# Lightning attention and an MLP on one Trainium2 core: plain row- and column-tiled attention for the first four chunks, and a static order planned for later landings of the early loads

## Chip, cores and metric

The kernel runs on one core of a Trainium2 chip. The metric is the device time of one execution in microseconds; lower is better. Time before: 229.05 us, the median of five runs (228.29 to 230.45).

## What is computed

Decayed linear attention over 4 batches, 8 heads, 768 positions and head size 64, followed by a two-layer MLP (512 to 2048 to 512) on the 3072 tokens that come out of it. The reference, cut to what matters:

```python
for b in range(nb):                       # blocks of 64 positions
    intra = np.einsum('bhic,bhjc->bhij', qb, kb) * Dmask[None]     # lam ** (i - j) for i >= j
    intra = np.einsum('bhij,bhjd->bhid', intra, vb)
    inter = np.einsum('bhid,bhde->bhie', qb * lam_pow[None], kv_state)
    out[:, :, sl] = intra + inter
    kv_state = lam_block[None, :, None, None] * kv_state + np.einsum('bhsd,bhse->bhde', kb * rev_pow[None], vb)
x = attn_out.transpose(0, 2, 1, 3).reshape(B * S, H * D)
h = x @ w_in
g = np.where(h >= 1, h, np.where(h <= -1, 0.0, (h + 1) ** 2 / 4))
return g @ w_out
```

## The kernel before

**Attention.** The 3072 tokens are 24 chunks of 128 tokens (c = 0 to 23), six to a batch; c0 or k0, q0, v0 below mean chunk 0 and its three loads. For each chunk the kernel loads k, q and v (each 128x512 f32, 256 KB), casts k and q to bf16 (`cast`, L246 on ACT, L248 on DVE for chunk 0), and multiplies v by a table of decays on POOL (`cast_v`, L252, into `vn`). TensorE then transposes k and q into one PSUM tile `pt` (`f_t`, L268). `f_kb` (L274) copies the transposed k out, `f_qT` (L278) multiplies the transposed q by the decay table `tab_q` (four pieces per two chunks, L141). The scores come in two steps g = 0 and 1: `f_s` (L294) is the product of k and q into the one PSUM tile `ps`, `f_m` (L300) multiplies by the causal mask into `sc`. `f_o` (L307, L310) adds the state's part and the scores times v into `po`, `f_x` (L317) casts `po` into a quarter of `xT`. `f_u` (L284) and `f_ub` (L288) keep the running state.

Two heads share the 128 partitions. To work on both with full-width matmuls the kernel lays k and v out block-diagonally: `kbd` and `vi` are zeroed once, and each chunk's data is written into the diagonal blocks, for `kbd` by two half-height copies, for `vi` by four small moves (`f_vb`: DVE copies at L260 for chunks 0 to 3, DMAs at L262 from POOL for chunks 4 to 11 and from SP behind them). Step g then covers the keys of one half of the chunk for both heads, so that step 1 needs only the later 64 queries.

**MLP.** The tokens are 6 stages of 512. `f_l1` (L327) is a group of 16 matmuls (or 8 twice as wide) of the first layer, 16 groups to a stage; `f_r` (L335) is the relu on ACT that empties its PSUM tile `ph` (two buffers); three DVE operations (L341, L345, L360) make `gT`; `f_l2` (L366) is a group of four 512-column matmuls of the second layer; `f_y` and `f_st` copy and store.

**The order.** Nothing is looped at run time. Every step is entered with `add(key, engine, ns, fn, needs, due, extra)`: its assumed duration, the time `extra` from its end until its result can be used, what it needs, and when it is due. `run_plan` then places the steps on the engines one by one, as a list scheduler does, and emits each engine's instructions in that order. On the chip each engine runs its own list in order; real waits come from data dependences alone. Where the plan leaves a gap on TensorE before the first l2, the kernel puts filler matmuls into the unused PSUM tile `spin` (L225).

**The loads.** A list `order` gives the sequence of chunk loads ("c") and of the eight weight pieces ("w": w0 to w3 are quarters of w_in, w4 to w7 of w_out; each 1 MB of f32, cast to bf16 by the DMA). Before, chunk 0's three loads and those of chunks 6 on are issued by SP, the weights and chunks 1 to 5 by POOL. The plan treats the DMA as one engine:

```python
add(key, "SP" if sp else "POOL", 600 if sp else 900 if kind == "c" else 800, fn, need, due=0, extra=1250 if sp else 930)
add(land, "DMA", ns, lambda: None, [key] + landed[-1:], extra=1000 if i < SW else 1500, due=0)
```

with ns = 2600 for a weight piece, 1060 for an SP load and 720 for a POOL load. The SP load of k of chunk 6 waits for the landing of w6 (`add_manual_dep`).

Of the kernel before, what the change touches and what calls it, by code (L numbers as in the profile page):

```python
# [8 lines left out]
F32 = mybir.dt.float32  # L9
# [14 lines left out]
def kernel(  # L24
# [30 lines left out]

    LD, RING = 6, 6
# [8 lines left out]
    scp = ctx.enter_context(tc.tile_pool(name="scp", bufs=3))  # L65
# [52 lines left out]
    nc.vector.memset(flat(kbd[0]), 0.0)  # L118
# [5 lines left out]
    nc.vector.tensor_scalar(causal, row[:, 0:128], late, None, op0=AX.is_ge)  # L124
    nc.vector.tensor_copy(row[:, 2 * C:], row_i[:, 2 * C:])
    for t in vi:
        nc.gpsimd.memset(flat(t), 0.0)  # L127
# [4 lines left out]
    ln_t = const.tile([128, HP], F32)  # L132
    for hi in range(2):
        nc.vector.tensor_copy(ln_t[64 * hi:64 * hi + 64], ln_lam[64 * hi:64 * hi + 64].rearrange("p (a b) -> p a b", b=2)[:, :, hi])
    tab_k = const.tile([128, NCB, H], F32)
    nc.scalar.activation(out=tab_k, in_=arg, func=AF.Exp, scale=-1.0)
# [35 lines left out]
    def run_plan(free):  # L172
# [14 lines left out]
        for x in reversed(topo):  # L187
            d = [u.due - u.ns - x.extra - LAT for u in users[x.key] if u.eng not in ("DMA", "SP")]
            x.due = min(d + ([x.own] if x.own is not None else []), default=1e9)
            if x.eng in ("DMA", "SP") or x.key[0] in ("l1", "l2", "li", "wi"):  # L190
                x.due = x.own
# [39 lines left out]
    def mm(*cols):  # L231
        return sum(c / 2.4 + 3 for c in cols)
# [24 lines left out]
    def f_vb(c, g, hi):  # L257
        o, i = vi[c % NV][HD[hi], :, g, hi, :], vn[c % NV][HD[g], :, hi, :]
        if c < CPS:
            nc.vector.tensor_tensor(o, i, i, op=AX.max)  # L260
        else:
            (nc.gpsimd if c < VP else nc.sync).dma_start(out=o, in_=i)  # L262
# [7 lines left out]
    KA = 2  # L270

    def f_kb(c, hi):
        e = nc.scalar.copy if c < KA else nc.vector.tensor_copy
        e(out=kbd[c % NKB][HD[hi], :, :, hi, :], in_=ptt[c][HD[hi], 1].rearrange("p a (b d) -> p a b d", b=2))  # L274
# [15 lines left out]
    def f_s(c, g):  # L290
        t = pp_s.tile([128, 4, 128], F32, name="ps", tag="ps")
        pst[c, g] = t if g == 0 else t[:, 0:2, :].rearrange("p a (b d) -> p (a b) d", b=2)
        for hp in range(HP):
            nc.tensor.matmul(pst[c, g][:, hp, :], lhsT=kbd[c % NKB][:, hp, g].rearrange("p a d -> p (a d)"),  # L294
                             rhs=qT[c][:, hp, 64 * g:], start=True, stop=True)

    def f_m(c, g):
        if g == 0:
            sc_sb[c] = [scp.tile([128, HP, n], BF16, name=f"sc{n}", tag=f"sc{n}") for n in (128, 64)]
        nc.vector.tensor_tensor(sc_sb[c][g], pst[c, g], _bc(causal[:, 0:128 - 64 * g], 1, HP), op=AX.mult)  # L300

    def f_o(c):
        cb = c % NCB
        po = pot[c] = pp_o.tile([128, HP, 128], F32, name="po", tag="po")
        for hp in range(HP):
            if cb > 0:
                nc.tensor.matmul(po[:, hp], lhsT=ubd[(c - 1) % NUB][:, hp, :], rhs=qT[c][:, hp, :],  # L307
                                 start=True, stop=False)
            for g in range(2):
                nc.tensor.matmul(po[:, hp, 64 * g:], lhsT=vi[c % NV][:, hp, g].rearrange("p a d -> p (a d)"),  # L310
                                 rhs=sc_sb[c][g][:, hp, :], start=(cb == 0 and g == 0), stop=(g == 1))
# [92 lines left out]
    def f_load(c, x):  # L404
        t = qkv_ld[c, x] = ld.tile([128, H, D], F32, name=f"x{x}f", tag=f"x{x}f")
        b, s0 = c // NCB, (c % NCB) * C
        e = nc.gpsimd if 0 < c < SW else nc.sync
        d = e.dma_start(out=t, in_=(q, k, v)[x][b, :, s0:s0 + C, :].rearrange("h p d -> p h d"))  # L408
        if c == SW and x == 1:
            tc.add_manual_dep(d.ins, w_dma[6].ins.name, SYNC)  # L410

    SW = 6
    order = [("c", 0), ("c", 1), ("w", 0), ("c", 2), ("w", 1), ("c", 3), ("w", 2), ("w", 3), ("w", 4), ("c", 4), ("w", 5), ("w", 6), ("c", 5), ("w", 7)]
    order += [("c", c) for c in range(6, NCH)]

    fifo, landed, splast = [], [], []
    for kind, i in order:
        for x in (1, 0, 2) if kind == "c" else (0,):
            sp = kind == "c" and not 0 < i < SW
            if kind == "w":  # L420
                key, land, ns, fn, need = ("wi", i), ("w", i), 2600, lambda i=i: load_w(i), []
            else:
                key, land, ns, fn = ("li", i, x), ("ld", i, x), 1060 if sp else 720, lambda i=i, x=x: f_load(i, x)
                need = [("cast", i - LD, x), ("w", 6) if i == SW else None]
# [8 lines left out]
            add(land, "DMA", ns, lambda: None, [key] + landed[-1:], extra=1000 if i < SW else 1500, due=0)  # L433
            landed.append(land)

    nz = {"kb": NKB, "ub": NUB, "vb": NV}
    for i in range(1, NKB):
        add(("z", "kb", i), "DVE", 540, lambda i=i: nc.vector.memset(flat(kbd[i]), 0.0))
    for i in range(NUB):
        add(("z", "ub", i), "DVE", 270, lambda i=i: nc.vector.memset(flat(ubd[i]), 0.0))  # L440

    for c in range(NCH):
        od, cb = o_due(c), c % NCB
        lastu = c - 1 if cb else c - 2
        for x in (1, 0):
            e = "DVE" if c == 0 else "ACT"
            add(("cast", c, x), e, 600 if e == "DVE" else 610, lambda c=c, x=x, e=e: cast(c, x, e),
                [("ld", c, x), ("t", c - 3), ("u", c - 3), ("cast", c - 1, x)])
        for hp in range(HP) if c < NCB and c % 2 == 0 else ():
            add(("tab", c, hp), "ACT", 410, lambda c=c, hp=hp: tabq(c, hp), [("tab", c, hp - 1)])  # L450
        add(("cast", c, 2), "POOL", 1060, lambda c=c: cast_v(c),
            [("ld", c, 2), ("o", c - NV), ("u", c - NV), ("cast", c - 1, 2)], due=-1)
        for i in range(4):
            need = [("cast", c, 2), ("o", c - NV), ("z", "vb", c)]
            if c < CPS:
                add(("vb", c, i), "DVE", 230, lambda c=c, i=i: f_vb(c, i // 2, i % 2), need)
            elif c < VP:
# [5 lines left out]
        for hi in range(2):  # L463
            add(("kb", c, hi), "ACT" if c < KA else "DVE", 480 if c < KA else 365, lambda c=c, hi=hi: f_kb(c, hi), [("t", c), ("s", c - NKB, 1), ("z", "kb", c)])
        add(("qT", c), "DVE", 690, lambda c=c: f_qT(c), [("t", c), ("o", c - 3), ("qT", c - 1)] + [("tab", c // 2 * 2, hp) for hp in range(HP) if c < NCB])
        if cb < NCB - 1:
            add(("u", c), "PE", mm(*[128] * 4), lambda c=c: f_u(c),
                [("cast", c, 1), ("cast", c, 2), ("ub", lastu, 0), ("ub", lastu, 1), ("u", lastu)], due=od - 6000, extra=FILL)
            for hi in range(2):
                add(("ub", c, hi), "ACT", 372, lambda c=c, hi=hi: f_ub(c, hi), [("u", c), ("o", c - NUB + 1), ("z", "ub", c)])  # L470
        for h in range(2):
            add(("s", c, h), "PE", mm(*[128 - 64 * h] * 4), lambda c=c, h=h: f_s(c, h),
                [("kb", c, 0), ("kb", c, 1), ("qT", c), ("m", c, 0) if h else ("m", c - 1, 1)],
                due=od - 5500 + 2000 * h, extra=FILL)
            add(("m", c, h), "DVE", 690 - 270 * h, lambda c=c, h=h: f_m(c, h), [("s", c, h), ("o", c - 3), ("m", c, 0) if h else None])
        add(("o", c), "PE", mm(*[128] * (8 if cb else 4), *[64] * 4), lambda c=c: f_o(c),
# [27 lines left out]
    run_plan({"PE": 5500, "ACT": 4900, "DVE": 4800, "POOL": 4100, "DMA": 2700, "SP": 800})  # L504
# [30 lines left out]
```

## Time and profile before

| | |
|---|---|
| median of 5 runs | 229.05 us (228.29 to 230.45) |
| the profiled execution | 230.45 us, its span 228.6 us |
| granted TensorE clock, mean | 0.993 |
| PE busy | 217.4 us (95%) |
| PE weight loads | 158.6 us (69%) |
| DVE / ACT / POOL busy | 161.8 / 138.4 / 70.3 us |
| HBM read / written | 27.27 / 6.29 MB |
| DMA, SP's hardware queue | 75,792 packets, 22.81 MB |
| DMA, POOL's software queue | 6,448 packets, 9.18 MB |
| filler matmuls (L225) | 37, 12.0 us |

The span runs from the first to the last instruction of the profiled execution; the rest of its time lies around it. Matmuls are pipelined and the profile counts each from issue to end, so PE can be busy without being at its peak. L numbers are lines of the kernel before.

### The profile page before, as it was taken

Reading aid. Unit: us, or ns where it says so; the run is one execution under the profiler, and the core shown is the slowest. Engines: PE = TensorE matmul, PEld = TensorE weight load, DVE = VectorE, ACT = ScalarE, POOL = GpSimd, SP = SyncE. Lnnn points to the kernel's source line nnn. Section 1 sums busy time; section 2 is a strip of 40 time slices with the busy share of each in tenths; the row PEclk is TensorE's granted clock in tenths of the full one; section 3 lists DMA queues with packets and bytes.
Section 4 is the critical chain, followed back from the end, with each engine's and each line's share of the span. In section 5 each row is a group of like instructions: output and inputs, shape, how many; then the busy total and the mean of one; then the engine's idle time right before and its main releaser. Section 6 shows DMA issues by size and latency. Waiting matters only on the chain.

```text
span 228.6 us, 5723 instructions
## 1 busy us (share of the span) xinstructions
PE 217.4 (95%) x2309; PEld 158.6 (69%) x2309; DVE 161.8 (71%) x295; ACT 138.4 (61%) x249; POOL 70.3 (31%) x91
## 2 busy tenths in 40 slices
PE   7679999999979999999999999999999999999993
PEld 2348898788667878787777677777777777766441
DVE  8785998985969995998577687584875775554300
ACT  3678785677777766767666567655565554545121
POOL 8987847666889140112011130000000000000000
PEclk9799999999999999999999999999999999999999
DMA  6999999999999999677975941112101101110212
GB/s 137 199 214 242 189 262 249 190 229 228 227 230 255 218 258 238 160 175 154 239 171 123 219 121 58 48 41 70 49 0 46 49 0 49 47 46 3 91 56 82
DMA packets 82410, 32.36 MB, mean 142 GB/s; under 512 B 73744, under 2 KB 77840, under 8 KB 82384
## 3 DMA queue, kind: packets, MB, share of 16 engines
q1 hardware_dynamic: 75792, 22.81, 40.7%
q0 software_dynamic: 6448, 9.18, 18.8%
q8 instruction: 18, 0.29, 0.5%
q14 instruction: 8, 0.07, 0.1%
q10 hardware_dynamic: 144, 0.00, 0.0%
HBM read 27.27 MB, written 6.29 MB: 147 GB/s over the span
## 4 chain that ended last, share of the span: by engine, by line
PE 75%; DMA 12%; POOL 7%; ACT 3%; issue 1%; DVE 0%; ACTq 0%; POOLq 0%
PE py L366 33%; PE ph L327 31%; DMA x1f<-in_k_dram 8%; DMA x2f<-in_v_dram 4%; PE pt L268 3%; PE ps L294 3%; PE po L310 3%; POOL vn L252 2%; PE po L307 1%; PE pu L284 1%; POOL x1f L408 1%; POOL x0f L408 1%; ACT r L335 1%; POOL vi L127 1%; POOL w_in_sb L154 1%
## 5 line engine op out<-in xcount | busy, mean ns | idle before, releaser
L327 PE MATMUL ph<-xT,w_in_sb 128*128 128x128 bf16 (+1 forms) x1152 | 98.9, 237 | 0.8 <-ACT xT L317 0.4
L366 PE MATMUL py<-w_out_sb,gT 128*128 128x512 bf16 x384 | 95.6, 379 | 0.0
L335 ACT ACTIVATE r<-ph,one 128x512 bf16<-128x512 f32 x96 | 65.4, 686 | 49.8 <-PE ph L327 36.4
L327 PEld LDWEIGHTS <-w_in_sb 128*128 128x128 bf16 x1152 | 81.6, 98 | 14.9 <-issue 1.3
L366 PEld LDWEIGHTS <-gT 128*128 128x128 bf16 x384 | 35.4, 98 | 27.7
L252 POOL TENSOR_TENSOR vn<-x2f,tab_k 128x512 bf16<-128x512 f32 x24 | 27.3, 1139 | 59.9 <-DMA vi<-vn 36.8
L341 DVE TENSOR_SCALAR t<-r 128x1024 bf16<-128x1024 bf16 x48 | 22.1, 461 | 31.9 <-ACT r L335 31.7
L345 DVE TENSOR_TENSOR w<-r,t 128x1024 bf16<-128x1024 bf16 x48 | 37.0, 771 | 1.3
L360 DVE TENSOR_TENSOR gT<-w,t 128x1024 bf16<-128x1024 bf16 x48 | 35.6, 741 | 1.3
L300 DVE TENSOR_TENSOR sc<-ps,causal 128x512 bf16<-128x512 f32 (+1 forms) x48 | 26.6, 554 | 9.6 <-PE ps L294 9.2
L371 ACT COPY osb<-py 128x512 f32<-128x512 f32 x24 | 14.0, 585 | 15.7 <-PE py L366 14.5
L274 DVE COPY kbd<-pt 64x512 bf16<-64x512 bf16 x44 | 18.4, 418 | 5.7 <-PE pt L268 5.3
L262 POOL DMA_DIRECT2D vi<-vn x32 | 20.2, 645 | 2.7 <-POOL vn L252 2.4
L294 PE MATMUL ps<-qT,kbd 128*128 128x128 bf16 (+1 forms) x192 | 16.2, 208 | 2.3 <-ACT kbd L274 1.2
L246 ACT CAST ks<-x1f 128x512 bf16<-128x512 f32 x23 | 14.2, 618 | 6.8 <-DMA x1f<-in_k_dram 4.6
L294 PEld LDWEIGHTS <-kbd 128*128 128x128 bf16 x192 | 12.6, 98 | 7.9 <-ACT kbd L274 2.6
L278 DVE TENSOR_TENSOR qT<-pt,tab_q 128x512 bf16<-128x512 bf16 x24 | 16.6, 691 | 0.7
L317 ACT CAST xT<-po 128x512 bf16<-128x512 f32 x24 | 14.0, 584 | 4.6 <-PE po L310 4.5
L288 ACT CAST ubd<-pu 64x256 bf16<-64x256 f32 x40 | 14.6, 365 | 2.8 <-PE pu L284 2.5
L310 PE MATMUL po<-sc,vi 128*128 128x128 bf16 x192 | 15.6, 206 | 0.3 <-DMA vi<-vn 0.3
L246 ACT CAST qs<-x0f 128x512 bf16<-128x512 f32 x23 | 14.2, 616 | 0.8 <-DMA x0f<-in_q_dram 0.8
L310 PEld LDWEIGHTS <-vi 128*128 128x128 bf16 x192 | 13.2, 98 | 1.6 <-DMA vi<-vn 0.5
(45 smaller groups left out, 130.4 us busy)
## 6 DMA issues: line engine op xcount, KB each, us to landing
out_dram<-osb SPq DMA_DIRECT2D x24, 256.0 KB, 2.0
x1f<-in_k_dram SPq DMA_DIRECT2D x19, 256.0 KB, 4.5
x0f<-in_q_dram SPq DMA_DIRECT2D x19, 256.0 KB, 4.5
x2f<-in_v_dram SPq DMA_DIRECT2D x19, 256.0 KB, 4.6
w_in_sb<-in_moe_w_in_dram POOLq DMA_DIRECT2D x4, 512.0 KB, 8.0
w_out_sb<-in_moe_w_out_dram POOLq DMA_DIRECT2D x4, 512.0 KB, 10.4
vi<-vn SPq DMA_DIRECT2D x48, 32.0 KB, 2.0
x1f<-in_k_dram POOLq DMA_DIRECT2D x5, 256.0 KB, 7.5
```

Source lines behind the costliest of these rows:

```text
L246: nc.scalar.copy(out=t, in_=qkv_ld[c, x])
L252: nc.gpsimd.tensor_tensor(vn[c % NV].rearrange("p a b d -> p (a b) d"), qkv_ld[c, 2], _bc(tab_k[:, c % NCB, :], 2, D), op=AX.mult)
L262: (nc.gpsimd if c < VP else nc.sync).dma_start(out=o, in_=i)
L294: nc.tensor.matmul(pst[c, g][:, hp, :], lhsT=kbd[c % NKB][:, hp, g].rearrange("p a d -> p (a d)"), rhs=qT[c][:, hp, 64 * g:], start=True, ...
L300: nc.vector.tensor_tensor(sc_sb[c][g], pst[c, g], _bc(causal[:, 0:128 - 64 * g], 1, HP), op=AX.mult)
L310: nc.tensor.matmul(po[:, hp, 64 * g:], lhsT=vi[c % NV][:, hp, g].rearrange("p a d -> p (a d)"), rhs=sc_sb[c][g][:, hp, :], start=(cb == 0 ...
L327: nc.tensor.matmul(ph[:, j * m:(j + 1) * m], lhsT=w_in_sb[:, ko, (i + j) * 128:(i + j + 1) * 128], rhs=xT[s][:, ko, p * m:(p + 1) * m], st ...
L335: nc.scalar.activation(out=r_t[grp][:, i, :], in_=ph_t[s, ni, part], func=AF.Relu, bias=one[:, 0:1])
L341: nc.vector.tensor_scalar(t_t[grp], r_t[grp], 0.5, 1.0, op0=AX.mult, op1=AX.min)
L345: nc.vector.tensor_tensor(w_t[grp], r_t[grp], t_t[grp], op=AX.subtract)
L360: nc.vector.tensor_tensor(o, w, t, op=AX.mult)
L366: nc.tensor.matmul(py_t[s, ms], lhsT=gT[s][:, ko, ms * 128:(ms + 1) * 128], rhs=w_out_sb[:, ko, :], start=(ko == 0), stop=(ko == FO - 1))
```

## The change

Chunks 0 to 3 (`PLAIN = 4`) no longer use the block-diagonal layout. Their transposed k is copied out as it stands (`kplain`, in one copy: ACT for chunk 0, DVE for 1 to 3), and step g of the scores is now head half g: four matmuls over 64 partitions (row-tiled) with all 128 queries. In `f_o` each pair of heads takes two matmuls with a 64-wide stationary operand straight from `vn`, into the two halves of the partitions of `po` (column-tiled). Their `vi` copies are gone, and both mask products are 128 wide, with a mask of their own (`plain`).

With that, the zeroing moves: `vi` is zeroed by POOL behind the cast of v1 instead of ahead of its first load, `kbd` by DVE after the last plain use, `ubd` in the preamble. The cast of `row` goes from DVE to ACT, `ln_t` is computed by ACT, `tab_k` is placed by the planner, and the later pieces of `tab_q` wait for kb of chunk 0 and x of chunk 1.

The load of v0 goes from SP to POOL, and so do those of chunk 6 (`SW = 7`). Chunk 4 stands ahead of w4, and w7 behind chunk 6; SP's first load behind them, k of chunk 7, waits for w7. The planner's durations, landing allowances and the engines' starting times change.

```diff
+    PLAIN, KA = 4, 1
...
-    nc.vector.memset(flat(kbd[0]), 0.0)
...
-    nc.vector.tensor_scalar(causal, row[:, 0:128], late, None, op0=AX.is_ge)
-    nc.vector.tensor_copy(row[:, 2 * C:], row_i[:, 2 * C:])
-    for t in vi:
-        nc.gpsimd.memset(flat(t), 0.0)
+    plain = const.tile([128, 128], F32)
+    for t, p in ((plain, pos[:, 0:1]), (causal, late)):
+        nc.vector.tensor_tensor(t, row[:, 0:128], ... p.to_broadcast([128, 128]), op=AX.is_ge)
+    for t in ubd:
+        nc.vector.memset(flat(t), 0.0)
+    nc.scalar.copy(out=row[:, 2 * C:], in_=row_i[:, 2 * C:])
...
-        if c < CPS:
-            nc.vector.tensor_tensor(o, i, i, op=AX.max)
-        else:
-            (nc.gpsimd if c < VP else nc.sync).dma_start(out=o, in_=i)
+        (nc.gpsimd if c < VP else nc.sync).dma_start(out=o, in_=i)
...
     def f_kb(c, hi):
-        e = nc.scalar.copy if c < KA else nc.vector.tensor_copy
-        e(out=kbd[c % NKB][HD[hi], :, :, hi, :], in_=ptt[c][HD[hi], 1].rearrange("p a (b d) -> p a b d", b=2))
+        if c < PLAIN:
+            (nc.scalar.copy if c < KA else nc.vector.tensor_copy)(out=kplain(c), in_=ptt[c][:, 1])
+        else:
+            nc.vector.tensor_copy(kbd[c % NKB][HD[hi], :, :, hi, :], ptt[c][HD[hi], 1].rearrange("p a (b d) -> p a b d", b=2))
+
+    def kplain(c):
+        return kbd[c % NKB][:, 0:2].rearrange("p a b c d -> p (a b c d)").rearrange("p (h k) -> p h k", k=128)
...
+        for i in range(4 if c < PLAIN else 0):
+            nc.tensor.matmul(t[:, i, :], lhsT=kplain(c)[HD[g], i, :], rhs=qT[c][HD[g], i, :], start=True, stop=True)
+        for hp in range(HP if c >= PLAIN else 0):
...
     def f_m(c, g):
+        if c < PLAIN:
+            t = scp.tile([128, HP, 128], BF16, name="sc128", tag="sc128")
+            sc_sb[c] = sc_sb.get(c, []) + [t]
+            nc.vector.tensor_tensor(t, pst[c, g], _bc(plain, 1, HP), op=AX.mult)
+            return
...
+            for hi in range(2 if c < PLAIN else 0):
+                nc.tensor.matmul(po[HD[hi], hp], lhsT=vn[c % NV][:, hp, hi, :], rhs=sc_sb[c][hi][:, hp, :],
+                                 start=(cb == 0), stop=True)
-            for g in range(2):
+            for g in range(2 if c >= PLAIN else 0):
...
-        e = nc.gpsimd if 0 < c < SW else nc.sync
+        e = nc.gpsimd if (c, x) > (0, 1) and c < SW else nc.sync
...
-            tc.add_manual_dep(d.ins, w_dma[6].ins.name, SYNC)
+            tc.add_manual_dep(d.ins, w_dma[7].ins.name, SYNC)
...
-    SW = 6
-    order = [("c", 0), ("c", 1), ("w", 0), ("c", 2), ("w", 1), ("c", 3), ("w", 2), ("w", 3), ("w", 4), ("c", 4), ("w", 5), ("w", 6), ("c", 5), ("w", 7)]
-    order += [("c", c) for c in range(6, NCH)]
+    SW = 7
+    order = [("c", 0), ("c", 1), ("w", 0), ("c", 2), ("w", 1), ("c", 3), ("w", 2), ("w", 3), ("c", 4), ("w", 4), ("w", 5), ("w", 6), ("c", 5), ("c", 6), ("w", 7)]
+    order += [("c", c) for c in range(7, NCH)]
...
-                key, land, ns, fn, need = ("wi", i), ("w", i), 2600, lambda i=i: load_w(i), []
+                key, land, ns, fn, need = ("wi", i), ("w", i), 2800, lambda i=i: load_w(i), []
...
-            add(land, "DMA", ns, lambda: None, [key] + landed[-1:], extra=1000 if i < SW else 1500, due=0)
+            add(land, "DMA", ns, lambda: None, [key] + landed[-1:], extra=950 if sp and i == 0 else 1000 if kind == "c" and i < 2 else 3500 if kind == "c" and i < SW else 2000, due=0)
...
+    for i in range(NKB):
+        last = max(c for c in range(PLAIN) if c % NKB == i)
+        add(("z", "kb", i), "DVE", 485, lambda i=i: nc.vector.memset(flat(kbd[i]), 0.0), [("s", last, 1)])
+    for i in range(NV):
+        add(("zv", i), "POOL", 530, lambda i=i: nc.gpsimd.memset(flat(vi[i]), 0.0), [("cast", 1, 2)], due=10 + i)
+    add(("tabk",), "ACT", 250, lambda: nc.scalar.activation(out=tab_k, in_=arg, func=AF.Exp, scale=-1.0))
...
-    run_plan({"PE": 5500, "ACT": 4900, "DVE": 4800, "POOL": 4100, "DMA": 2700, "SP": 800})
+    run_plan({"PE": 5500, "ACT": 4450, "DVE": 4650, "POOL": 2250, "DMA": 2700, "SP": 800})
```

## The prediction

> **What bounds the kernel now.** I read four views in this order: the windows (cut where the matter changes), the same windows for the filler matmuls of L225 alone, the chain that ended last, and the timeline of the first 18 us with the landing of each load.
>
> The windows; columns are busy us with (count) for PE, PEld, DVE, ACT, POOL, then granted clock, DMA share, GB/s:
>
> ```profile
> 0.00:17.35 17.35, 12.21 (x74) 5.83 (x75) 13.77 (x33) 10.78 (x23) 15.36 (x25) 0.90 0.85 183
> 17.35:30.00 12.65, 12.54 (x196) 11.06 (x196) 10.21 (x23) 10.13 (x21) 10.37 (x12) 1.00 1.14 222
> 30.00:45.00 15.00, 15.00 (x214) 12.38 (x211) 13.87 (x25) 10.63 (x19) 9.20 (x13) 1.00 1.08 229
> 45.00:70.00 25.00, 22.98 (x314) 18.31 (x312) 19.43 (x33) 17.84 (x35) 19.13 (x27) 1.00 0.97 229
> 70.00:211.00 141.00, 141.00 (x1457) 105.06 (x1456) 102.66 (x181) 86.08 (x150) 16.27 (x17) 1.00 0.46 113
> ```
>
> and of L225 alone:
>
> ```profile
> 0.00:17.35 17.35, 9.35 (x26) 2.94 (x26) 0.90 0.85 183
> 17.35:30.00 12.65, 2.70 (x11) 0.99 (x11) 1.00 1.14 222
> ```
>
> Much early PE time is filler, and busy time overlaps. So I counted work from start to start: a 128-column matmul in a stream takes 56 ns of PE, a 64-column one 30, a 512-column one 216. That gives 203.1 us of needed work in the span of 228.65, and 25.5 us in which PE did none: 15.0 before the first l1 at 17.35, 2.8 from there to 30, none to 45, 3.2 from 45 to 70, 0.3 to 211, and 4.3 behind the last matmul. From 70 us on PE is full, so the end moves by what is lost before 70, and by nothing else.
>
> The chain says what PE waited for:
>
> ```profile
> 15.17 8.57 DMA x2f<-in_v_dram
> 23.82 1.33 POOL vn L252
> ...
> 52.57 5.24 DMA x1f<-in_k_dram
> 57.89 0.62 ACT ks L246
> ...
> 61.01 5.84 DMA x1f<-in_k_dram
> 66.93 0.62 ACT ks L246
> ```
>
> Loads: v of chunk 3, later k of chunks 9 and 11. In the last two, ACT stood at a cast written into its order before the data could be there, with the relus that empty PSUM for PE behind it. The timeline of the start:
>
> ```profile
> 2.16 1.92 POOL L127 MEMSET vi<- 128x512 f32 x4
> 2.27 1.89 DVE L124 TENSOR_SCALAR causal<-row,late 128x128 f32<-128x128 f32 x1
> 4.03 1.07 POOL L408 DMA_DIRECT2D x1f<-in_k_dram  x1
> ...
> 9.57 1.17 ACT L274 COPY kbd<-pt 64x512 bf16<-64x512 bf16 x2 [1.79 <-DVE qT L278]
> ...
> 17.35 1.05 PE L327 MATMUL ph<-xT,w_in_sb 128*128 128x128 bf16 x16 [0.38 <-ACT xT L317]
> ```
>
> The memsets of vi hold POOL, and with it the first POOL load, until 4.03. L124 runs as long as they do. The first l1 waits for x of chunk 0, although its weights, w0, landed at 15.39: 2 us are the attention's, the rest the loads'.
>
> **What the order was written for.** Summing the old code's load durations, the order expects w0 at 11.7, v2 13.8, w1 16.4, v3 18.6, w3 23.8, v5 35.9. They landed at 15.39, 17.67, 20.14, 23.75, 28.77, 41.26, so 4 to 5 us late. The new constants expect w0 12.5, v2 16.4, w1 17.7, v3 21.6, w3 25.7, v4 29.6, w4 30.9, v5 40.4, w7 44.1.
>
> **Part 1, start of the loads.** Without the memsets POOL is free at 2.2 (ident ends at 2.22), so its first DMA starts 1.8 us earlier; it is now v0, moved from SP to POOL and ahead of k1. Each POOL load costs 0.9 of issue (966, 914, 897 ns), so v0, k1, q1, v1 are issued by 5.9 and w0 by 6.7 (before 7.62). DMA packets run almost without a break from 2 us to 39, so not all of the 1.8 is won. k0, q0 and so far v0 are 1,040 packets of at most 256 B each, moved at about 1,030 a microsecond; on POOL's queue a load is 64 packets of 4 KB, and v1 landed 0.86 us after q1. At 4.0 k0 is moved and 455 packets of q0; 0.6 for its other 585, four POOL loads at 0.85 and 0.6 from the last packet to the landing give 8.6 for v1, against 9.94. With slower loads (0.97) it is 9.1. I take 1.0 us earlier for all early loads: w0 14.3, w1 19.1, w3 27.7.
>
> The price is q0. Between 43.5 and 44.75 the packet records show POOL's 1 KB packets and SP's 256 B ones one for one, about 38 of each per quarter microsecond, where SP alone has 260 to 280. q6, issued at 39.53, landed at 46.59. POOL's first packets followed its first issue by 1.7 us, so now they come near 4.0, when those 585 packets are still to go. One for one against 4 KB packets they get 65 to 250 a microsecond: q0 lands between 6.5 and 10.5, not at 5.22. I take 8.5, nearer the one-for-one row. Behind its cast on DVE stand t, kb and qT of chunk 0.
>
> **Part 2, attention of chunks 0 to 3.** DVE loses 16 vi copies (4.5 us), the row cast of 1.96 (to ACT, about 0.6 by the 0.62 casts of that width) and the two ln_t copies, so the k0 cast moves from 5.92 to about 4.8. It gains a mask (128x128, off the path before 4.3) and 4 x (0.69-0.41) = 1.1 us in the wider second mask product. kb of chunk 0 is one ACT copy of 0.58 for two; chunk 1 has a DVE copy of 0.42 for ACT's 1.17; chunks 2 and 3 save one copy each. From qs to x the old chain of chunk 0 took 8.06 to 17.30, of which 2 us were kb behind qT and m1 and o waiting behind chunk 1. I expect qs 8.5-9.2, t 9.8, kb and qT one after the other 11.2, s and m twice 13.6, o 14.4, x 15.1: first l1 near 15.5, 1.85 us earlier. The vi memsets (4 x 0.52 on POOL) now lie behind the cast of v1, ahead of some loads; with several loads in flight that costs nothing, and up to 2 us if the queue runs dry. The kb memsets (3 x 0.485) go behind the last plain s, beside PE work. tab_k is now placed by the planner and POOL's vn(0) waits for it; at 5 us on ACT it is ahead of v0. The tables of chunks 2 and 4 now stand behind kb(0) and x(1) on ACT, which puts kb(0) ahead of 1 to 2 us of them.
>
> PE pays: s is 8 x 56 for 4 x 56 + 4 x 30, 0.10 more; o the same 0.10. Of the 0.8 us half lies in idle time before 15.5; 0.4 counts. Changes of tile shape come on top: two for each s, two for chunk 0's o, eight for the others', 42 in all, 24 of them in chunks 2 and 3 where PE is nearly full. No row shows one. Nearest from below: neighbours of one shape, 0. From above: a matmul that nothing overlaps shows 220 ns instead of 56, 0.16. I take 0.04, near zero because the trace's changes between full-width operations cost nothing: 24 x 0.04 = 1.0; bounds 0 and 3.9. Pairs of half-width matmuls running side by side could return 0.7.
>
> The Trainium skill, "TensorEngine Tiling (Array Packing)", Key Properties, says that changing the tiling mode drains the engine, which speaks against this change. If a drain showed the whole 0.16, the sum below would be 2.9 us worse. No row of before has a mode change.
>
> **Part 3, order of the loads.** c4 before w4 brings v4 from 33.92 to about 30.1 and w4 from 31.52 to 32.6; l1 of stage 1 (first at 45.3) can start near 39. c6 goes from SP to POOL (3 x 0.9 of issue, beside waits), ahead of w7. SP's next load, k7, waits for w7: about 45.1. All later loads and the stores are queued behind it. A lone SP load took 3.5 us (k6), so k7 lands at 48.6 against 49.70: no loss.
>
> **The sum.** First stage: -1.85. From there to about 28: work is there for 12.0 of 12.2 us but comes in steps (w1 19.1, w2 25.2), so I put 1.4 lost, -1.4. To 45 the weights come barely ahead of PE, +0.4. From 45 to 70: k9 is expected at 58.0 where the old order had 52.2, and should land earlier than 57.81, so ACT should rarely stand; I take half of 3.2, -1.6, bounds 0 and -3.2. PE's own +1.4. Together -3.05. The profiled execution was 230.45 with 1.80 outside its span, and would be 227.4 with a span of 225.6; it is the slowest of the five shown, 1.40 over the median. On the median 229.05: 226.0.
>
> **Rivals.** (1) DMA is full anyway and nothing lands earlier, and the wait from 45 to 70 stays: first l1 at 15.6 for w0 at 15.39 gives -1.75, PE +1.4: 228.7. For: DMA share 1.14 in the second window. Against: 4 KB packets and a start 1.8 us earlier. (2) q0 starves past 10.5: x of chunk 0 at 17 as before, -1.85 lost: 227.9. For: q6 above. (3) Slower: changes of tile shape drain PE in chunks 2 and 3, 0.25 us for each of 24: 6.0 for 1.0, 231.0. It decides from (3.05 + 1.0)/24 = 0.17 each. For: nothing hides PE there after 17 us. Against: the filler, 2.70 us there, would give way first.
>
> **How the numbers follow.** Forecast 0.66 (alone 223.4 to 227.8), rival 1 0.14, rival 2 0.12, rival 3 0.08. A measurement of this kernel can tell about 0.5%, 1.15 us, from no change: faster is below 227.9. Faster: most of the forecast and half of rival 2, 0.73; same: most of rival 1 and the other half, 0.16; slower 0.11. The best case (45 to 70 all won, no drains) is 223.4; low 222.8 leaves room for side-by-side tiles. High 229.0 takes in rivals 1 and 2.
>
> **What would show it.** Right: first POOL load issued near 2.2; q0's cast on DVE later than 7; first l1 at 14.5 to 16.5; filler behind it below 2.7; w7 landed by 45.5; no ACT idle over 1 us before ks between 45 and 70; PE busy in 45:70 over 23.7. Wrong: gaps between the s and o matmuls of chunks 2 and 3; POOL's loads issued no earlier; new ACT or DVE waits between 28 and 45.

## The result, and the profile after

The changed kernel takes 0.9976 of the time before, with an interval of 0.9959 to 0.9993: medians 229.04 us of 38 runs (226.78 to 232.42) against 229.96 us of 75 runs (227.22 to 232.05). On the 229.05 us that the forecast started from, that is 0.55 us less: inside the range (228.5), but "the same" where 226.0 was forecast. The profiled execution took 229.52 us with a span of 227.7, against 230.45 and 228.6. Every ratio here and below is of the fast runs alone, because some executions of each kernel fall into a slower state; the medians in us are of all executions.

The windows of the changed kernel, in the columns shown for before:

```profile
0.00:17.35 17.35, 14.63 (x105) 7.64 (x106) 9.11 (x22) 11.79 (x27) 16.44 (x27) 1.00 0.90 212
17.35:30.00 12.65, 12.65 (x179) 10.24 (x177) 9.24 (x16) 9.33 (x19) 10.58 (x13) 1.00 1.14 235
30.00:45.00 15.00, 15.00 (x218) 12.54 (x216) 13.66 (x21) 10.61 (x20) 11.24 (x16) 1.00 0.98 206
45.00:70.00 25.00, 24.39 (x321) 18.98 (x319) 21.12 (x37) 17.07 (x33) 16.23 (x24) 1.00 0.93 216
70.00:211.00 141.00, 139.63 (x1439) 103.90 (x1437) 103.05 (x181) 85.77 (x151) 17.81 (x19) 1.00 0.46 113
```

and of the filler alone, which is now L227:

```profile
0.00:17.35 17.35, 9.39 (x29) 3.02 (x30) 1.00 0.90 212
17.35:30.00 12.65, 2.07 (x9) 0.46 (x6) 1.00 1.14 235
```

In the second window PE is busy all the time, with less filler than before, and yet it starts 179 matmuls, 9 of them filler, where before started 196 with 11: that is where the gain went. In 45:70 PE is busy 24.39 us for 22.98. In 70:211 it is no longer full: 139.63 for 141.00.

The same count as in the prediction (start to start, 56, 30 and 216 ns a matmul) gives the time in which PE did no needed work, in us. The half-width matmuls of o run side by side in pairs, which makes up for the wider s, so the needed work stays at 203.1 us.

| window | before | after | difference | forecast |
|---|---|---|---|---|
| 0 to 17.35 | 15.00 | 13.54 | -1.46 | -1.85 |
| 17.35 to 35 | 2.65 | 4.31 | +1.66 | 0.0 (-1.4 and +1.4) |
| 35 to 45 | 0.10 | 0.04 | -0.06 | +0.4 |
| 45 to 70 | 3.18 | 0.92 | -2.26 | -1.6 |
| 70 to 211 | 0.30 | 1.76 | +1.46 | 0 |

The start, from the timeline of the changed kernel (start, duration, and in brackets the wait before it):

```profile
2.17 1.07 POOL L420 DMA_DIRECT2D x2f<-in_v_dram  x1
2.47 0.29 DVE L126 TENSOR_TENSOR causal<-row,late 128x128 f32<-128x128 f32 x1
...
5.54 0.69 DVE L250 TENSOR_TENSOR qs<-x0f 128x512 bf16<-128x512 f32 x1 [0.21 <-DMA x0f<-in_q_dram]
...
6.75 0.58 ACT L271 COPY kbd<-pt 128x512 bf16<-128x512 bf16 x1 [0.62 <-PE pt L267]
...
14.07 1.07 PE L339 MATMUL ph<-xT,w_in_sb 128*128 128x128 bf16 x16 [0.59 <-DMA w_in_sb<-in_moe_w_in_dram]
```

POOL issues its first load at 2.17, the mask takes 0.29 us for 1.89, q0 is cast at 5.54 and not at 8.5, and the first l1 comes at 14.07, now waiting for its weights alone. It is 3.28 us earlier than before, but only 1.46 us of that is left at 17.35: from 14.07 to there PE spends 1.03 us on filler and 0.90 on the eight changes of tile shape in o of chunk 1. Landings: w0 14.02 (before 15.39), w1 18.99 (20.14), w3 26.78 (28.77), v4 29.02 (33.92).

### The profile page after: what moved, and what is told of

The parts are those of the page before. It is cut to its first block, busy times and chain, and to the rows that moved or that the text cites. A ratio compares the mean times of both kernels' runs of the same rounds, so it can differ in the third digit from the quotient of the medians.

```text
span 227.7 us, 5693 instructions
## 1 busy us (share of the span) xinstructions
PE 219.3 (96%) x2308; PEld 159.0 (70%) x2308; DVE 158.0 (69%) x276; ACT 136.9 (60%) x249; POOL 72.3 (32%) x95
## 4 chain that ended last, share of the span: by engine, by line
PE 81%; DMA 5%; SPq 4%; DVE 4%; POOL 2%; issue 1%; ACT 0%; POOLq 0%; ACTq 0%
PE ph L339 33%; PE py L378 33%; PE pt L267 4%; DMA w_in_sb<-in_moe_w_in_dram 4%; PE ps L298 3%; SPq L261 3%; PE po L322 2%; PE po L316 2%; DMA vi<-vn 2%; SPq L420 2%; PE pu L286 2%; DVE gT L372 1%; DVE w L357 1%; PE py L227 1%; PE po L319 1%; POOL x2f L420 1%
## 5 line engine op out<-in xcount | busy, mean ns | idle before, releaser
L378 PEld LDWEIGHTS <-gT 128*128 128x128 bf16 x384 | 34.6, 98 | 27.5
L254 POOL TENSOR_TENSOR vn<-x2f,tab_k 128x512 bf16<-128x512 f32 x24 | 25.9, 1077 | 59.7 <-PE ps L298 16.9
L372 DVE TENSOR_TENSOR gT<-w,t 128x1024 bf16<-128x1024 bf16 x48 | 38.0, 793 | 1.1
L353 DVE TENSOR_SCALAR t<-r 128x1024 bf16<-128x1024 bf16 x48 | 22.4, 466 | 23.2 <-ACT r L347 22.7
L357 DVE TENSOR_TENSOR w<-r,t 128x1024 bf16<-128x1024 bf16 x48 | 36.1, 752 | 1.4
L309 DVE TENSOR_TENSOR sc<-ps,causal 128x512 bf16<-128x512 f32 (+1 forms) x40 | 22.1, 553 | 7.7 <-PE ps L298 7.5
L273 DVE COPY kbd<-pt 64x512 bf16<-64x512 bf16 x40 | 16.8, 419 | 9.3 <-PE pt L267 9.0
L322 PE MATMUL po<-sc,vi 128*128 128x128 bf16 (+1 forms) x160 | 13.2, 206 | 1.4 <-DMA vi<-vn 1.4
L298 PE MATMUL ps<-qT,kbd 128*128 128x128 bf16 (+1 forms) x160 | 13.3, 206 | 0.6 <-DVE qT L280 0.6
L316 PE MATMUL po<-qT,ubd 128*128 128x128 bf16 x80 | 13.7, 221 | 0.0
L298 PEld LDWEIGHTS <-kbd 128*128 128x128 bf16 x160 | 10.5, 98 | 3.4 <-issue 0.6
```

What stands on the lines that cost most here:

```text
L254: nc.gpsimd.tensor_tensor(vn[c % NV].rearrange("p a b d -> p (a b) d"), qkv_ld[c, 2], _bc(tab_k[:, c % NCB, :], 2, D), op=AX.mult)
L353: nc.vector.tensor_scalar(t_t[grp], r_t[grp], 0.5, 1.0, op0=AX.mult, op1=AX.min)
L357: nc.vector.tensor_tensor(w_t[grp], r_t[grp], t_t[grp], op=AX.subtract)
L372: nc.vector.tensor_tensor(o, w, t, op=AX.mult)
L378: nc.tensor.matmul(py_t[s, ms], lhsT=gT[s][:, ko, ms * 128:(ms + 1) * 128], rhs=w_out_sb[:, ko, :], start=(ko == 0), stop=(ko == FO - 1))
```

## What the runs tell apart

Three theories of where the rest went. **D**: every change of tile shape drains PE, at about 0.105 us. **S**: SP issues too many things one after the other, and a move of vi comes late behind them (the wait at 111 us, below). **C**: the chain of chunk 2, with its later l1 groups, is bound by its loads and not by PE. Each time is given as a ratio to the kernel before; 0.001 is 0.23 us, and the changed kernel stands at 0.9976.

### Changes of tile shape

PE in the o step of chunk 2, from the timeline of the kernel before and then of the changed one:

```profile
18.24 0.22 PE L307 MATMUL po<-qT,ubd 128*128 128x128 bf16 x1
18.30 0.25 PE L310 MATMUL po<-sc,vi 128*128 128x128 bf16 x2
18.38 0.22 PE L307 MATMUL po<-qT,ubd 128*128 128x128 bf16 x1
18.44 0.25 PE L310 MATMUL po<-sc,vi 128*128 128x128 bf16 x2
```

```profile
22.79 0.22 PE L316 MATMUL po<-qT,ubd 128*128 128x128 bf16 x1
22.94 0.25 PE L319 MATMUL po<-sc,vn 128*64 128x128 bf16 x2
23.12 0.23 PE L316 MATMUL po<-qT,ubd 128*128 128x128 bf16 x1
23.28 0.25 PE L319 MATMUL po<-sc,vn 128*64 128x128 bf16 x2
```

No wait is shown for a matmul, and the durations agree to 0.03 us. But a pair of heads takes 0.14 us before and 0.34 after: 0.15 to 0.16 from the full-width matmul to the half-width pair (0.056 without a change), 0.18 back. So a change costs 0.09 to 0.12, on average 0.105 us over all changes of this profile (those around the row-tiled s steps 0.09 to 0.10). Busy time hides it, since the matmul ahead counts as running; only the spacing of starts shows it, and the weight loads (PEld) of the same stretches, again before and then changed:

```profile
18.25 0.15 PEld L310 LDWEIGHTS <-vi 128*128 128x128 bf16 x2
18.36 0.10 PEld L307 LDWEIGHTS <-ubd 128*128 128x128 bf16 x1
```

```profile
22.94 0.11 PEld L319 LDWEIGHTS <-vn 128*64 128x64 bf16 x2 [0.27 <-issue]
23.11 0.10 PEld L316 LDWEIGHTS <-ubd 128*128 128x128 bf16 x1
```

Before, a load starts 0.03 to 0.05 us ahead of its matmul, under the matmul in front; behind a change it starts within 0.004 us of its own matmul. Whether the 0.105 us are PE draining or a load of 0.1 us that nothing covers, these runs don't tell, and "drain" stands for either here.

**Eight plain chunks.** 48 more changes, where PE is full.

```diff
-    PLAIN, KA = 4, 1
+    PLAIN, KA = 8, 1
```

> The changed kernel with plain attention for the first eight chunks instead of four. It doubles the suspected cost where PE is full: 48 more changes of tile shape in chunks 4 to 7, 105 ns each, 5.0 us; chunk pairs of half-width matmuls return 0.1 us each, and 16 vi moves of POOL and their latency go. Theory D: 3 to 5 us slower than the change (232 to 234). Rival: the moves of vi that go are worth as much, within 1 us.

Measured 1.0149 (1.0098 to 1.0200), 233.09 us: 1.73% or 4.0 us over the changed kernel, 0.083 us for each change if nothing else differs. D holds.

**Two plain chunks.** Chunks 2 and 3 go back to block-diagonal attention:

```diff
-    PLAIN, KA = 4, 1
+    PLAIN, KA = 2, 1
...
+        if c < CPS:
+            nc.vector.tensor_tensor(o, i, i, op=AX.max)
```

(`vi` of chunks 2 and 3 is zeroed by DVE in the preamble.)

> The changed kernel with plain attention for chunks 0 and 1 alone; chunks 2 and 3 block-diagonal as before, with DVE copies of v and zeroing beside other work. It takes 24 of 42 changes of tile shape away (2.5 us of PE at 105 ns each) and puts 8 DVE copies of 0.28 us and the two-part k copies back. Theory D (the changes of shape gave the early gain back): PE without work from 17 to 35 us falls by 1.5 to 2.5, time 226.5 to 228. Rival C (what PE waits for there is the chain of chunk 2 from its landing to x, 8.7 us long whatever the tiling): within 0.5 us of the change, or slower for the DVE work.

Measured 0.9932 (0.9895 to 0.9969), 228.21 us: 1.0 us below the changed kernel (good to some 0.9), the lower end of what D asked for.

**Two plain chunks, o grouped.** The same, and in chunk 1 the four full-width matmuls of o come first, then the eight half-width ones: 2 changes instead of 8.

```diff
+            for hp in range(HP if cb > 0 else 0):
+                nc.tensor.matmul(po[:, hp], lhsT=ubd[(c - 1) % NUB][:, hp, :], rhs=qT[c][:, hp, :],
+                                 start=(hp == 0), stop=True, skip_group_check=True)
+            for hp in range(HP):
+                for hi in range(2):
+                    nc.tensor.matmul(po[HD[hi], hp], ... start=(cb == 0), stop=True, ...)
```

> Plain attention for chunks 0 and 1 alone, and in chunk 1's o step full-width matmuls first: 12 changes of tile shape instead of 42, 3.2 us of PE less. With two plain chunks and eight changes in that o step the time was 0.993 of before. Theory D: 0.990 to 0.993 of before. Rival (chunk 1's six fewer changes lie beside PE's idle time): 0.993 to 0.996.

Measured 0.9917 (0.9880 to 0.9954), 226.84 us, span 225.7: the fastest of all. It beats the changed kernel by 0.6%, 1.4 us.

**The changes alone.** Two plain chunks differ from four in DVE's work and in the chain of chunk 2 too. So this run keeps the kernel just shown and adds matmuls of one column and half width, behind each s step and each head pair of o in chunks 2 and 3, into the filler's PSUM:

```diff
+    def flip(c):
+        if c in (2, 3):
+            nc.tensor.matmul(spin[0:64, 0:1], lhsT=idle[:, 0:64], rhs=idle[:, 0:1], start=True, stop=True)
```

> This is the kernel with two plain chunks and grouped o (0.9917 of before), with twelve half-width matmuls of one column written into the filler's PSUM added in chunks 2 and 3: one behind each of the two s steps and one behind each of the four head pairs of o. They put 24 changes of tile shape back, and nothing else of the plain tiling. Theory D (the changes of shape drain PE, about 0.105 us each by the starts of matmuls in the trace of the changed kernel): 24 x 0.105 = 2.5 us if nothing hides them, 1.3 if half falls into waits; ratio to before 0.997 to 1.002. Theory C (the two chunks gain because the chain of chunk 2 is shorter or the work is done by another engine, not because of the drains): within 0.5 us of the kernel without them, 0.990 to 0.994.

Measured 1.0021 (0.9991 to 1.0051), 229.94 us. That is 1.04% or 2.4 us above the kernel without them (the two were set against before in different sets of runs, so the difference is good to some 1.1 us). D said 1.3 to 2.5; C, at most 0.5, falls. Its timeline:

```profile
23.57 0.22 PE L333 MATMUL po<-qT,ubd 128*128 128x128 bf16 x1
23.63 0.25 PE L339 MATMUL po<-sc,vi 128*128 128x128 bf16 x2
23.80 0.19 PE L297 MATMUL py<-idle 128*64 128x1 bf16 x1
23.93 0.23 PE L333 MATMUL po<-qT,ubd 128*128 128x128 bf16 x1
```

Here the one-column matmul starts 0.12 us behind the matmul ahead of it and the next one 0.12 us behind it, and the group of 0.14 us lasts 0.36. No run adds the same matmuls at full width, so what a short matmul costs by itself isn't taken off; the changed kernel adds none, and its spacings give the same price.

**Fewer changes in the changed kernel.** The grouping of o shown above, in chunks 1 to 3 of the changed kernel: 18 changes fewer, 12 of them in chunks 2 and 3.

> The changed kernel, but in the plain o step of chunks 1 to 3 the four full-width matmuls come first and the eight half-width ones behind them: two changes of tile shape instead of eight. In the trace of the change a step from one shape to the other takes 150 to 177 ns instead of 56. Theory D (the early gain was given back to these changes, in chunks 2 and 3, where PE has no other wait): six changes fewer in each of two steps, 12 x 0.11 = 1.3 us off the time, and PE without work between 20 and 35 us falls from 3.9 to 2.6. Rival W (PE waits for loads and casts there anyway): the o steps get shorter and the time stays within 0.3 us.

Measured 0.9975 (0.9934 to 1.0016), 228.30 us: nothing gained, where D asked for 1.3 us. In its profile o of chunk 2 takes 0.65 us instead of 1.35, so the changes were saved; but w1 landed at 20.51, 1.5 us later than in the profile of the changed kernel, and PE waited 1.44 us for it:

```profile
20.56 1.07 PE L348 MATMUL ph<-xT,w_in_sb 128*128 128x128 bf16 x16 [1.44 <-DMA w_in_sb<-in_moe_w_in_dram]
```

With w0 it waited 2.55 us for weights, where the changed kernel waited 0.59, and still it had lost no more by 35 us (17.9 us for 17.8). So in that execution the saving was there, and late weights took it. A gain up to 1.0 us lies within the interval of the twelve. That it isn't seen in them is a miss for D which these runs don't explain.

**No filler placed behind 13.4 us of the plan.**

```diff
-                for _ in range(int((t - pe_end - 60) // (216 if t > 8000 else 430))):
+                for _ in range(int((t - pe_end - 60) // (216 if t > 8000 else 430)) if t < 13400 else 0):
```

> The changed kernel without filler matmuls that the plan puts behind 13.4 us (about 14 of them, 3 us of PE). In the change six of them stand on PE from 16.3 to 17.8 us although the transposes of chunk 2 could begin near 17.0. Theory F (filler stands in the way of work): 0.7 to 1.2 us faster. Rival: PE would wait anyway, within 0.4 us; or the granted clock falls below 1.00 between 15 and 30 us and it is slower.

Measured 0.9987 (0.9944 to 1.0030): no gain is seen, and of the 0.7 to 1.2 us that the filler was suspected of, the interval leaves some 0.7.

### What the start, the order and the allowances are worth

**All three, no plain chunk.** The `vi` and `kbd` buffers are zeroed by DVE, and its `vi` copies of chunks 0 to 3 are back.

```diff
-    PLAIN, KA = 4, 1
+    PLAIN, KA = 0, 2
...
+        if c < CPS:
+            nc.vector.tensor_tensor(o, i, i, op=AX.max)
```

> The changed kernel with no plain chunk: early start, new sequence and new allowances, block-diagonal attention throughout, vi copies of the first chunks on DVE. It tells what plain attention is worth. Theory D with no other effect (each plain chunk costs PE its drains): below the kernel with two plain chunks, 0.985 to 0.992. If plain attention of chunks 0 and 1, which lie before the first l1 where PE has room, saves DVE time on the chain to x of chunk 0, above it: 0.994 to 1.000, with the first l1 0.5 to 1.5 us later than 14.1.

Measured 0.9940 (0.9915 to 0.9965), 228.33 us. In its profile the first l1 comes at 15.64, 1.6 us later than with plain attention, and no more time is lost from 17.35 to 35 (3.62 us) than in the changed kernel (4.31). So start, order and allowances gain 0.6%, 1.4 us, and plain attention of four chunks gives 0.8 us of that back (good to some 0.7). Two plain chunks cost nothing that these runs can show.

**The early start taken away.** `vi` is zeroed by POOL ahead of its loads again, and the plan's POOL starts later.

```diff
+    for t in vi:
+        nc.gpsimd.memset(flat(t), 0.0)
...
-    run_plan({"PE": 5500, "ACT": 4450, "DVE": 4650, "POOL": 2250, "DMA": 2700, "SP": 800})
+    run_plan({"PE": 5500, "ACT": 4450, "DVE": 4650, "POOL": 4150, "DMA": 2700, "SP": 800})
```

> The changed kernel with the zeroing of vi on POOL ahead of the loads again, as before the change; the plan knows it (POOL free at 4.15). All early loads land some 1.5 us later. If PE in the first 35 us is bound by landings, the time rises by about as much, 230.3 to 231. If it is bound by the chain of the chunks and the written order, less than 0.6 us.

Measured 1.0145 (1.0070 to 1.0221), 234.35 us: by the ratios 3.9 us over the changed kernel (good to some 1.8), where later landings alone were put at 1 to 2. In its profile PE also waits 3.2 us for moves of vi, so more than the start may be in it.

**The early start alone.** The kernel without a plain chunk, with the old sequence, durations and allowances.

```diff
-    SW = 7
+    SW = 6
...
-... ("w", 3), ("c", 4), ("w", 4), ("w", 5), ("w", 6), ("c", 5), ("c", 6), ("w", 7)]
+... ("w", 3), ("w", 4), ("c", 4), ("w", 5), ("w", 6), ("c", 5), ("w", 7)]
...
+... extra=1000 if i < SW else 1500, due=0)
```

> The changed kernel with no plain chunk (attention is block-diagonal throughout, with the vi copies of the first chunks on DVE), the old load sequence and the old allowances: of the change only the early start of the loads is left, with the vi and kb buffers zeroed by DVE. If the early start wins by itself what the first stage shows (1.5 us), 0.992 to 0.995. If it needs the new allowances (the changed kernel with the old ones stood at 1.014, with ACT standing at casts placed too early), 1.005 to 1.015.

Measured 1.0184 (1.0138 to 1.0230), 234.28 us, above both forecasts.

**The allowances taken away.**

```diff
-... extra=950 if sp and i == 0 else 1000 if kind == "c" and i < 2 else 3500 if kind == "c" and i < SW else 2000, due=0)
+... extra=1000 if i < SW else 1500, due=0)
```

with the old durations (2600, 720).

> The changed kernel with the old durations and landing allowances in its plan (weights 2600, chunks 720, allowance 1000 or 1500); load order, attention and start as changed. If the allowances mended the stage from 45 to 70 us, ACT again stands idle for k casts there, the stage loses 2 us or more and the time is 230.5 to 231.5. Rival: the order of the loads mended it, and the time is within 0.5 us of the change. If later allowances cost more before 45 us (filler planned ahead of data) than they save behind it, it is faster than the change.

Measured 1.0143 (1.0071 to 1.0216), 231.51 us. In its profile 45 to 70 is as good as in the changed kernel (0.92 us lost) and 17.35 to 35 is not (6.85 for 4.31). Two things are late there. Its ACT, from the timeline:

```profile
24.78 0.58 ACT L329 CAST xT<-po 128x512 bf16<-128x512 f32 x1 [3.04 <-PE po L319]
25.26 1.27 ACT L347 ACTIVATE r<-ph,one 128x512 bf16<-128x512 f32 x2
```

The first l1 runs from 16.94 to about 18.8 here, but its relu stands until 25.26, behind the x of a chunk whose landing was planned earlier; in the changed kernel it starts at 15.18, as its l1 ends. And the clock, from the windows of this kernel (granted clock third from the right):

```profile
13.00:15.00 2.00, 1.21 (x13) 0.64 (x13) 1.18 (x2) 1.43 (x3) 1.96 (x3) 1.00 1.00 200
15.00:17.00 2.00, 1.92 (x17) 0.98 (x16) 1.02 (x2) 0.66 (x2) 1.67 (x2) 0.76 1.19 228
17.00:19.00 2.00, 2.00 (x21) 1.80 (x20) 0.00 (x0) 1.95 (x5) 2.00 (x4) 0.50 1.04 335
19.00:21.00 2.00, 2.00 (x21) 1.80 (x19) 0.69 (x1) 1.29 (x4) 0.66 (x1) 0.50 1.19 187
21.00:23.00 2.00, 2.00 (x13) 1.07 (x12) 0.76 (x2) 0.72 (x2) 1.53 (x2) 0.53 1.22 198
23.00:25.00 2.00, 2.00 (x21) 1.15 (x19) 0.42 (x1) 0.22 (x1) 2.00 (x4) 1.00 1.20 254
```

Behind a stretch in which PE is busy 1.21 us of 2.00, the granted clock is 0.50 for some 6.8 us (16.0 to 22.9): at most 3.4 us of PE's time. Four of the six executions show a mean clock of 0.982 to 0.985 and took 230.79 to 233.07 us; the two at 1.0 took 229.78 and 230.99. So the clock and the order both have a part in what the old allowances cost; six executions don't say which is the larger.

**The allowances alone**, with the new durations, on the kernel before.

```diff
-... extra=1000 if i < SW else 1500, due=0)
+... extra=950 if sp and i == 0 else 1000 if kind == "c" and i < 2 else 3500 if kind == "c" and i < SW else 2000, due=0)
```

> The kernel before with the new durations and landing allowances alone; load sequence, preamble and attention stay. The kernel with the new sequence as well stood at 1.014. If the allowances cost by themselves on the old late start (the order is planned for landings that come later than planned anyway, and everything that hangs on a cast is put behind), 1.008 to 1.014. If the sequence with chunk 4 ahead of w_out costs that, 0.995 to 1.002, because the stage from 45 to 70 us is mended by the allowances.

Measured 1.0053 (1.0019 to 1.0086), 230.35 us. DVE in its profile:

```profile
21.14 0.49 DVE L341 TENSOR_SCALAR t<-r 128x1024 bf16<-128x1024 bf16 x1 [4.69 <-ACT r L335]
21.55 0.84 DVE L274 COPY kbd<-pt 64x512 bf16<-64x512 bf16 x2
```

With k2 planned to be usable later, the first MLP step t stands ahead of kb of chunk 2. On the old late start the relu it needs comes only at 20.4, DVE waits 4.69 us, and the attention of chunk 2 waits behind it. 45 to 70 is mended here too (0.74 us lost).

**Allowances and sequence on the kernel before.** The edit just shown, and:

```diff
-    SW = 6
+    SW = 7
...
-... ("w", 3), ("w", 4), ("c", 4), ("w", 5), ("w", 6), ("c", 5), ("w", 7)]
+... ("w", 3), ("c", 4), ("w", 4), ("w", 5), ("w", 6), ("c", 5), ("c", 6), ("w", 7)]
```

> The kernel before with only the order of the loads (chunk 4 ahead of w4, chunk 6 on POOL ahead of w7) and the new durations and landing allowances of weights and chunks in the plan; attention, zeroing and the engine that loads v of chunk 0 as before. If the stalls between 45 and 70 us came from an order written for too early landings, ACT's idle time before its k casts goes and that stage wins about 2.3 us, as in the change, with the start as before: first l1 near 17.4, time 226.5 to 228.5. Rival: the stalls were the loads' own lateness, which only the earlier start mends: the time stays within 0.5 us of before.

Measured 1.0138 (1.0080 to 1.0197), 231.49 us, slower than either forecast: 45 to 70 is mended, but its profile loses 5.4 us from 17.35 to 35, for 2.65 before.

**The sequence taken away.** The last edit undone, in the changed kernel:

```diff
-    SW = 7
+    SW = 6
```

> The changed kernel with the old sequence of loads (w4 ahead of chunk 4, chunk 6 on SP behind w6, w7 behind chunk 5); allowances, attention and start as changed. Theory O (the sequence mended the stage from 45 to 70 us: with the old allowances it lost 0.9 there, as the change does, and 3.2 before): that stage loses 2 us or more again, and the time is 230.5 to 231.5. Rival: the sequence also brings w7 2.2 us later than before (48.3 for 46.0) and costs as much as it mends: within 0.5 us of the change.

Measured 0.9995 (0.9962 to 1.0028), 229.42 us; in its 45 to 70 ACT waits for no cast either. So sequence or allowances, each alone, mend that stage.

### Behind 70 us

The chain of the changed kernel between 92 and 114 us:

```profile
104.67 1.01 SPq L261
...
107.17 4.16 DMA vi<-vn
111.32 0.14 issue
111.46 0.19 PE po L322
```

SP issues loads and the four moves of vi in one list; this move takes 4.16 us to land, and PE waits 1.37 us for it:

```profile
111.46 0.19 PE L322 MATMUL po<-sc,vi 128*128 128x64 bf16 x1 [1.37 <-DMA vi<-vn]
```

**More slack in the plan for SP's moves of vi.**

```diff
-... "SP", 600, lambda c=c, i=i: f_vb(c, i // 2, i % 2), need, due=-0.5, extra=2200)
+... "SP", 600, lambda c=c, i=i: f_vb(c, i // 2, i % 2), need, due=-0.5, extra=4200)
```

> The changed kernel, but the plan allows SP's small vi moves (chunks 12 on) 4.2 us until their landing instead of 2.2. In the change PE stands 1.37 us at 110 us for one that took 4.16 us. Theory S (a new wait, because the plan trusted the move to land in 2.2 us): that wait goes, 1.2 to 1.5 us off the time. Rival: o then stands later in PE's list and another step waits in its place, or PE lacks work elsewhere: within 0.4 us.

Measured 1.0023 (0.9985 to 1.0062), 229.47 us. The wait is absent from its profile, and the time is no better.

**More vi moves on POOL.**

```diff
-    VP = 12
+    VP = 16
```

> The changed kernel, but POOL instead of SP issues the vi moves of chunks 12 to 15. In the change SP's list is the chain from 94 to 107 us (eight moves at 0.68 us each, then a store, loads and four more moves), and PE stands 1.37 us at 111 for the last of them. Theory S (between 70 and 115 us SP's list, not PE, sets the pace, and takes back what is won before): 1 to 2 us faster than the change. Rival: the wait at 111 belongs to one execution, or POOL's moves disturb DVE as much: within 0.5 us.

Measured 1.0077 (1.0037 to 1.0117), 231.06 us: slower, where S asked for 1 to 2 us less. PE's waits behind 70 us in its profile (us in total, times, longest):

```profile
PE ps L298 <- DVE sc L309: 1.7, 2, 1.3
PE ps L298 <- DVE qT L280: 0.3, 1, 0.3
```

No move of vi is waited for any more, but DVE is. So the edit puts one wait in the place of another, and neither of these two runs shows that SP sets the pace of the median kernel.

**The same edit on the fastest kernel.**

> The same, and POOL issues the vi moves of chunks 12 to 15. Theory D and S together: 226 to 227.5, 0.984 to 0.990 of before. If only D holds 0.990 to 0.994; if later stages take back what the start wins, 0.995 or more.

Measured 0.9959 (0.9922 to 0.9996), against 0.9917 without it: no gain from the moves on POOL here either.

## Why the prediction was wrong

**Right.** The loads on POOL start 1.8 us earlier, and those from w0 to v3 land 1.1 to 2.8 us earlier (w0, w1 and w3 within 1 us of the forecast); v4 was put at 30.1 and landed at 29.02. No ACT wait over 1 us stands before a ks from 45 to 70. PE there is busy 24.39 us, over the 23.7 asked for. The first l1 is better than forecast (14.07 for 15.5): both rivals in which the start wins less (loads no earlier, q0 starved) fall.

**The step that failed first: the price of a change of tile shape.** The prediction took 0.04 us between bounds of 0 and 0.16, near zero because changes between full-width operations cost nothing in the trace. It is 0.105: 24 changes in chunks 2 and 3 are 2.5 us for 1.0. And eight more, in o of chunk 1, which the sum did not count, came behind the first l1 and cost 0.9 us; the first stage won 1.46 for 1.85 although the first l1 came 1.4 us earlier than forecast. The rows say the same: the gaps between needed matmuls from 17.35 to 35 went from 0.3 to 2.7 us. So the stage lost 1.66 where the terms -1.4 and +1.4 should have met, and the lead of 2.4 us at the fourth relu (22.7 for 25.2) lies between -0.1 and 2.0 from the ninth to the sixteenth (0.4 there, 42.4 for 42.8). Nor did the filler give way: from the first l1 to 35 us it is 2.6 us, where the kernel before has 2.4. The rival that priced this at 0.25 had the mechanism and not the size: at 0.105 it didn't decide alone. The rule weighed there (the Trainium skill, "TensorEngine Tiling (Array Packing)", Key Properties, that changing the mode drains the engine) agrees with these runs, which put 0.105 us on it; the sum should have gone by the upper half of its bounds.

**A step that holds in some executions only: "from 70 us on PE is full, so the end moves by what is lost before 70, and by nothing else".** In the profile 1.46 us more than before were lost there, most of it at 111. Other kernels lose there too, at other places: without plain chunk 1.36 us (0.9 of it a wait for DVE's mask product), with sequence and allowances alone 2.1. But in the profiles of four others (fewer changes, old allowances, added changes, allowances alone) PE is busy 141.00 of these 141.00 us, as before; fewer changes has the same SP list as the changed kernel. That this one wait costs the median kernel its time isn't shown, since slack removed it and gained nothing.

**Mis-sized or misplaced.** The term for 45 to 70 was -1.6 and measured -2.26, but it was credited to the allowances; the sequence does it as well. What the allowances buy lies before 35 us (+1.7% without them, part of it a clock that stood at half for 6.8 us), and only with the early start, as the early start wins only with them. The prediction summed the parts one by one; alone the start costs 1.8% and the allowances 0.5%, and with the sequence they gain 0.6% together.

**Smaller misses.** q0 landed at 5.51, not 8.5: POOL's first packet came at 4.40, 2.2 us after its issue, when 586 of the 1,040 packets of q0 were moved, and POOL moved only 18 packets until 5.0, so the one-for-one row didn't apply. k1, q1 and v1 land only 0.2 to 0.6 us earlier than before (v1 at 9.59, put at 8.6). w7 landed at 48.27 for 45.1, issued at 39.81 behind the three loads of chunk 6, and k7 at 51.37 for 48.6; no wait of PE in that profile leads back to either. The side-by-side pairs, named as a possible return of 0.7, start 2 to 4 ns apart, so a plain o needs 0.12 us less than before, where the prediction had it 0.10 more, and s and o together cost no more.

**Open.** The stages of the two profiled executions sum to -0.9 with the tail, the medians say -0.55, and executions of one kernel spread over 2%: a loss under 1 us behind 70 us can't be placed. Nor is the fewer-changes run explained.

## What to carry to other kernels

Price a change of PE's tile shape by the spacing of starts, not by busy time or waits, and keep the shapes together: half-width tiles cost nothing where PE had idle time and lost where it had none, and the best version here used them in the first two chunks alone. A static order and the landings that it is planned for are one change: with earlier loads under the old plan, or a new plan over the old loads, every kernel here was slower than before. Where PE has no slack, check in more than one execution that the other engines' lists hold behind the stage that is mended.

## What the runs showed that was not expected

A change of tile shape costs 0.09 to 0.12 us each way even for a matmul of one column, and the profile shows no wait of the matmul for it; its traces are the spacing of starts and a weight load that starts only with its own matmul.

Products on VectorE stretched where POOL's cast of v fell into them. From the timeline of the changed kernel, VectorE and then POOL:

```profile
40.11 2.11 DVE L357 TENSOR_TENSOR w<-r,t 128x1024 bf16<-128x1024 bf16 x1
42.25 0.69 DVE L372 TENSOR_TENSOR gT<-w,t 128x1024 bf16<-128x1024 bf16 x1
```

```profile
40.59 1.08 POOL L254 TENSOR_TENSOR vn<-x2f,tab_k 128x512 bf16<-128x512 f32 x1
```

The product that meets POOL's cast of v takes 2.11 us, the next one of the same shape 0.69. Of the 96 products of this shape nine take over 0.8 us (1.13 to 2.11), all of them where such a cast falls in; the kernel before has as many.

With the old allowances the granted clock fell to half behind a stretch in which PE was busy 1.21 us of 2.00 (13 to 15 us), and stayed there for 6.8 us of busy PE; in the changed kernel, with 1.41 busy, it stayed at 1.00. But the kernel before was less busy still and kept its clock:

```profile
13.00:15.00 2.00, 0.80 (x4) 0.19 (x2) 1.54 (x5) 1.16 (x2) 2.00 (x3) 1.00 1.00 247
15.00:17.00 2.00, 1.90 (x23) 1.24 (x24) 1.46 (x4) 1.92 (x5) 1.08 (x2) 1.00 1.02 201
```

So the busy share of that stretch doesn't decide it, and why the clock fell isn't shown. The Trainium skill, "TensorE: Matmul & The Clock Gate", Part 1, has the clock at half after at least one idle window and back after at least one busy window of about 3.4 us; the 6.8 us here are about two such windows.

Weights with the same early code landed between 12.4 and 14.9 us (w0) and between 17.8 and 21.4 us (w1) in the profiled executions, so one trace's landing is good to a microsecond or two.
